# Small operations off VectorE, a re-ordered head and bracketed 64-row tails in a transformer block on one core

## The chip, the core and the metric

The kernel runs on one core of a Trainium2 chip. The metric is the device time of one execution in microseconds (us); lower is better. The core has five engines that run side by side, each with its own queue that it works through in order: TensorE (PE in the profile, its weight loads PEld), VectorE (DVE), ScalarE (ACT), GpSimd (POOL) and SyncE (SP), which here issues nearly all DMA transfers.

## The reference

The input is x, 2048 rows of 576. A block with attention and a feed-forward network is computed in two halves, each behind a layer norm and with a residual.

```
h  = x + A(layernorm(x))                 # A: 32 heads of 18, 4 segments of 512 rows
h2 = h + gelu(layernorm(h) @ w1 + b1) @ w2 + b2      # w1: 576 x 4608
# in A, for each segment s, with q, k, v of that segment:
p    = softmax(q k^T * 18**-0.5, causal inside the segment)
dot  = p @ v
mem  = (phi(q) @ M) / (phi(q) @ z + 1e-6)    # phi(t) = t+1 if t>0 else exp(t)
o    = g * mem + (1-g) * dot                 # g = sigmoid(beta), per head
M   += phi(k)^T v ;  z += sum of phi(k)      # for the next segment
A    = concat(o) @ wo
```

Data are bfloat16; sums are kept in float32.

## The kernel before

The rows are worked in 8 chunks of 256, each of two tiles of 128 rows. A segment is two chunks. Per tile: the layer norm (`layernorm`, L725 to L760) has its statistics, a sum and a product on DVE (L729, L733 to L735), a power on POOL (L740) and the application on DVE or ACT (L743, L748). The normalised tile `xn1` is transposed to `xT`, on PE for the first two tiles (L761) and by a transposing DMA after that (L491). Four projections of 432 columns, each five matmuls (L722 for the four full rows of 128, L723 for the rest of 64 rows and a row of zeros), give Q, K and V, which ACT or DVE copies out of PSUM (L844 to L854). Q and K are transposed in turn (L874 on PE, else L491).

The attention (`stream_A`) goes in 80 visits. A visit runs 16 score matmuls of 32 rows, four at a time on PE (L957), into the four-bank tile `st4`; ACT takes the exponential of all 128x2048 (L974); POOL masks the blocks on the diagonal (L978); later PE multiplies with V (L997) into the bank `ox`, and DVE and POOL finish (L1043 to L1053). From the second segment on, the memory is recalled (`memory_in`, `memory_mm`, L1011 to L1034) from `MZ_blk`, which DVE makes from the sums `MZacc` (L933, L936). `stream_B` multiplies with wo, adds the residual, norms again to `xn2` (with a copy of its last 64 columns, L745) and transposes to `xn2T`.

The feed-forward part is two streams. `stream_F1` takes w1 in groups of 512 columns (`load_w1`), 9 groups per chunk and 72 in all, in two buffers `w1g` (the first five groups lie elsewhere too). A group of 128 columns of the hidden layer over 256 rows is five matmuls: four with 128 rows (L722) and one with the last 64 rows and a row of zeros (L723), which runs in full mode like the others. Its sum is evicted with the bias by DVE or ACT (`evict`, L1286 and L1284), and gelu is taken by ACT over many at once (L1349), with a table load when ACT comes from the exponential. `stream_F2` multiplies with w2 (L1376). A `Pair` is another form of the same work: two halves of a w1 group, whose four 64-row rests (`tail`, L1214) run two at a time in the upper and lower half of PE, put ahead of a visit's scores, since PE changes its tile mode there anyway; the full parts (`main`, L1220) follow. PE's banks are three plus, before and after the attention, `ox`.

The order of all of it is made when the program is built. Each piece of work is an `op` on an engine with an assumed duration and a due time (`SLACK`, `PHASES`, and the recorded due times `LATE`); `step` plays through time, and on each engine begins the ready operation that is due first:

```
can = [o for o in queue[e] if o.ready() <= now and not (e == "SP" and waits_for_queue(o))]
if can:
    begin(min(can, key=lambda o: (o.due, o.made)))
```

PE takes what the streams offer. Where PE would have nothing to do early on (`WARM`, the first 62 us of the plan), a matmul of zeros is put in (L1424), which then stands in PE's queue like any other. On the chip the queues run in that fixed order and wait for each other by semaphores. `either` chooses between DVE and ACT for an eviction by what each has queued.

Of the kernel before, what the change touches and what calls it, by code (L numbers as in the profile page):

```python
# [8 lines left out]
ACT = mybir.ActivationFunctionType  # L9
# [7 lines left out]
def kernel(  # L17
# [41 lines left out]
    def sbuf(name, shape, dt=BF16):  # L59
# [13 lines left out]
    SLACK = dict(head=2.35, lnp=15.71, lnb=4.06, pow=-3.98, apply=7.94, ek_k=78.96, relu_k=-8.71, min_k=3.71,  # L73
                 add_k=10.93, mz=14.56, exp=16.96, ek=21.6, relu=47.98, min=14.06, add=31.72, hb=57.84,
                 gelu=30.88, finish=-1.23, mem=0.08, sum=20.21, out=3.91, hd=34.06, xp=-29.81, xb=-19.31,
                 t_x=23.19, t_q=37.57, t_k=38.16, t_o=-3.03, t_h=19.9, w1=3.76, w2=33.77, hc=-2.46, evict=-17.31,
                 qk=7.8, ot=-7.54, mask=0.42, lead=1.57, balance=22.63, b1=11.77, zeros=6.77, hold=0.62,
                 delay=0.92, pe_x=2, pe_q=3, pe_k=2, pe_o=2, pe_h=1, d_x1=1.69, d_wk=-5.24, marg=0.8, cj=4,
                 flex=1.0, qkv=0.0, flexn=1.0, d_wv=1.68, d_xb=0.5, d_wo=3, d_b2=1.97, bulk=11.07, w2v=5)
    PHASES = [(30.0, dict(exp=38.12, hold=2.18, sum=8.51, lnp=15.18, min_k=9.68, lead=1.93, t_h=47.5, t_o=-3.5,  # L80
                          flexn=1.85, mem=25.71)),
              (60.0, dict(gelu=28.89, apply=7.66, min_k=-36.61, lnp=16.16, w2=14.91, qk=8.17, t_q=37.57, delay=0,
                          hc=9.3)),
              (110.0, dict(t_x=30.47, min=14.15, mz=13.94, hold=5.27, w1=24.51, t_q=28.42, ek=20.74, apply=0.43,
                          pow=-9.03, xp=-16.35, hc=0.85, w2=31.47, out=4.0, bulk=8.26)),
              (200.0, dict(mem=-1.42, w1=12.55, lead=3.33, t_o=-5.89, mask=8.5, finish=-0.41, xb=-20.35, hd=32.92,
                          lnb=4.83, exp=20.2, apply=21.55)),
              (300.0, dict(add_k=6.54, delay=0.17, add=4.0, hd=24.4, mem=3.13, mz=15.86, ek_k=80.69, min_k=14.3,
                          exp=16.63, join=-18.57, qk=4.56, lead=1.87, xp=-30.24, min=9.66, qkv=5.33, t_x=21.9,
                          out=37.08, apply=10.19, hold=0.28))]  # L90
# [81 lines left out]
    def note(o, rd, wr):  # L172
# [5 lines left out]
        for k in rd:  # L178
# [4 lines left out]
        'wqkv0': [0.2],  # L183
        'mhalf': [4.1],
        'wqkv_pad': [4.4],
# [14 lines left out]
        ('x_p', 0): [0, 15.2, 41.5, 77.3, 169.5, 193.4, 233.4],  # L200
        ('qk', 0, 'pad'): [17.5],
        'wqkv1': [1.4],
        ('v1', 0): [22.7],
        ('v1', 1): [26.9],
        'ident': [4.9],
        ('v1', 2): [45.5],
        ('v1', 3): [57.3],
        'wqkv1t': [1],
        ('v1', 4): [60.2],
        ('v1', 5): [67.5],  # L210
        'maskcol': [58.4, 70.6, 62.4, 71.3, 63.8],
        ('qk', 2, 'pad'): [24.9],
        ('x_p', 1): [2, 26.1, 91.6, 103.7, 202.6, 212.6, 294.4],
        ('v1', 6): [123.5],
        'beta': [29.3],
        'wqkv2': [3.5],
        'wqkv2t': [3.7],
        ('o', 0, 'pad'): [27.9],
        ('x_b', 0): [7.6, 30.5, 71.9, 119, 172.9, 230.9, 273.1, 317.9, 377.7],
        ('phik', 0, 'pad'): [32.7],  # L220
        ('wo', 4): [38.2, 44],
        ('phik', 1, 'pad'): [33.8],
        ('w1', 0, 'z', 0): [41.5],
        ('x_b', 1): [10.9, 45, 87.4, 133.1, 201.2, 242.8, 296.4, 330.6, 418],
        ('w1', 0, 'z', 1): [39.6],
        'stp0': [2.8, 3.3, 3.8, 4.3, 11, 11.5, 11.9, 12.5, 21.5, 23.3, 21.5, 22.3, 51.2, 47.3, 36.4, 25.7,
            78.9, 94.5, 95.4, 97.9, 174.1, 174.5, 175, 175.5, 195.3, 194.5, 193.8, 196.7, 244.8, 239.6,
            247.2, 236.5],
        ('w1', 1, 'z', 0): [44.9],
        'b1': [18.1],  # L230
        ('w1m', 2, 'z', 1): [46.3],
        ('wo', 0): [23.5],
        ('w1m', 2, 'z', 0): [59],
        ('w1', 1, 'z', 1): [53.3],
        ('qk', 3, 'pad'): [57.8],
        ('o', 1, 'pad'): [48.3],
        ('xn1', 0): [5, 13.2, 25.8, 49.4, 89.7, 176.2, 197.5, 238.4],
        ('w1m', 3, 'z', 1): [58.4],
        ('w1m', 3, 'z', 0): [58.7],
        ('w1m', 4, 'z', 1): [66],  # L240
        ('xT', 'p', 0): [5.2, 16.9, 22.9, 46.4, 90.3, 177.4, 198.5, 245.7],
        'MZb': [71.1, 69, 72.3, 71.4, 71.7, 76.8, 64.6, 74.2, 62.6, 191.3, 192.4, 192.2, 195.4, 196.6, 197.4,
# [1240 lines left out]
```

## Time and profile before

| | |
|---|---|
| time, median of 3 runs | 478.51 us (477.85 to 479.26) |
| the profiled execution: time | 476.5 us |
| its span | 474.8 us, 14410 instructions |
| busy DVE, ACT, POOL | 311.4, 302.9, 217.2 us |
| matmuls on PE | 6056, of these 76 fillers with zeros |
| granted PE clock | 1.00 |
| HBM read, written | 60.09 MB, 7.08 MB |

The profile is of one execution. A group of its table 5 reads: line, engine, operation, output and input tiles, shapes, count | busy time in us, mean of one in ns | idle time of the engine before them and what ended it. In the timeline, a row is start, length, engine, line, operation, count and, in brackets, idle time before it. Matmuls are pipelined: a row's length is longer than the time until the next can start.

### The profile page before, as it was taken

The page shows a single profiled execution, that of the slowest core. Times are in us where ns is not written, and L with a number is a line of the kernel's source. Part 1 is how long each engine was busy: PE and PEld are TensorE (multiplying, and loading weights), DVE is VectorE, ACT ScalarE, POOL GpSimd, SP SyncE. Part 2 cuts the span into 40 slices and gives each one's busy share as a digit, 9 for nine tenths or more (in the row PEclk, how much of TensorE's full clock was granted, in tenths as well). Part 3 has the DMA queues.
Part 4 walks back from the last instruction along what each step waited for, and adds up shares of the span by engine and source line. Part 5 has one row for each costly group of instructions (what it writes and reads, how often), then busy time and mean ns, then how long its engine had stood idle before and what let it go on. Part 6 is the DMA issues. An engine that isn't in the chain of part 4 may idle for free.

```text
span 474.8 us, 14410 instructions
## 1 busy us (share of the span) xinstructions
PE 462.5 (97%) x6056; PEld 350.9 (74%) x6056; DVE 311.4 (66%) x744; ACT 302.9 (64%) x245; POOL 217.2 (46%) x333
## 2 busy tenths in 40 slices
PE   8999999799999999999999999999999999999997
PEld 6655687468777777767768777777877788888875
DVE  4889996587877476888877556887457646334310
ACT  2578879964678668896789595687457864212210
POOL 9468463295745344786773518665133312000000
PEclk9999999999999999999999999999999999999999
DMA  8999799927588577469458559486744655655411
GB/s 240 200 231 206 262 163 295 253 52 165 162 214 218 150 178 185 97 142 199 83 155 204 156 143 193 89 196 187 181 147 135 185 166 158 185 168 164 137 39 50
DMA packets 118881, 79.94 MB, mean 168 GB/s; under 512 B 53344, under 2 KB 116768, under 8 KB 118816
## 3 DMA queue, kind: packets, MB, share of 16 engines
q1 hardware_dynamic: 118784, 79.01, 66.8%
q8 instruction: 47, 0.77, 0.7%
q14 instruction: 18, 0.15, 0.1%
q0 software_dynamic: 32, 0.01, 0.1%
HBM read 60.09 MB, written 7.08 MB: 141 GB/s over the span
## 4 chain that ended last, share of the span: by engine, by line
PE 84%; DVE 6%; ACT 4%; issue 2%; DMA 2%; SPq 1%; ACTq 0%; DVEq 0%
PE bank L722 29%; PE bank L1376 26%; PE bank L723 7%; PE st L957 5%; PE ox L997 4%; PE bank L1220 4%; PE ox L1376 3%; PE st L1424 2%; DMA xT<-xn 2%; ACT pt L974 1%; PE ox L722 1%; PE bank L1026 1%; ACT hT L1349 1%; DVE ox L1043 1%; PE bank L1214 1%
## 5 line engine op out<-in xcount | busy, mean ns | idle before, releaser
L974 ACT ACTIVATE pt<-st 128x2048 bf16<-128x2048 f32 x80 | 150.2, 1877 | 65.4 <-PE st L957 63.6
L1376 PE MATMUL bank<-w_sb,hT 128*128 128x288 bf16 x1044 | 144.0, 286 | 2.1 <-ACT hT L1349 2.1
L1286 DVE TENSOR_TENSOR hT<-bank,b1T 128x512 bf16<-128x512 f32 x130 | 89.3, 688 | 72.5 <-PE bank L723 65.1
L1376 PEld LDWEIGHTS <-hT 128*128 128x128 bf16 x1152 | 110.5, 98 | 31.8 <-ACT hT L1349 2.4
L978 POOL TENSOR_SCALAR_AFFINE_SELECT pt<-pt 128x512 bf16<-128x512 bf16 x128 | 80.4, 643 | 107.1 <-ACT pt L974 105.4
L722 PE MATMUL bank<-xn2T,w1g 128*128 128x256 bf16 (+1 forms) x888 | 122.2, 269 | 1.9 <-DMA w1g<-in_B_w_dram 0.9
L722 PEld LDWEIGHTS <-w1g 128*128 128x128 bf16 x944 | 88.4, 98 | 16.3 <-issue 1.5
L1349 ACT ACTIVATE hT<-hT 128x4608 bf16<-128x4608 bf16 (+5 forms) x23 | 66.0, 2874 | 46.7 <-DVE hT L1286 46.5
L723 PE MATMUL bank<-xn2T,w1g 128*128 128x256 bf16 (+1 forms) x222 | 59.7, 269 | 0.0
L722 PE MATMUL bank<-wqkv,xT 128*128 128x432 bf16 x256 | 57.4, 346 | 1.1 <-DMA xT<-xn 0.8
L722 PEld LDWEIGHTS <-xT 128*128 128x128 bf16 x384 | 34.9, 97 | 23.7 <-DMA xT<-xn 0.9
L1016 POOL TENSOR_TENSOR pq<-ek,pq 128x512 bf16<-128x512 bf16 x24 | 27.9, 1163 | 11.8 <-DVE ek L1014 9.1
L957 PE MATMUL st<-QT,KT 32*128 32x128 bf16 x1280 | 32.2, 217 | 1.2 <-ACT pt L974 1.1
L1043 DVE STREAM_TRANSPOSE ox<-ox 128x512 f32<-128x512 f32 x32 | 23.2, 725 | 11.7 <-PE ox L997 11.1
L1380 DVE TENSOR_TENSOR ot<-bank,hc 128x288 bf16<-128x288 f32 x29 | 13.1, 453 | 25.1 <-PE bank L1376 25.1
L957 PEld LDWEIGHTS <-KT 32*128 32x128 bf16 x1280 | 18.8, 92 | 14.3 <-issue 9.2
L997 PE MATMUL ox<-pt,v_aug 128*19 128x128 bf16 x1280 | 26.5, 220 | 0.0
L997 PEld LDWEIGHTS <-v_aug 128*19 128x19 bf16 x1280 | 17.9, 91 | 10.9 <-issue 10.0
L723 PEld LDWEIGHTS <-w1g 128*128 128x128 bf16 x236 | 23.1, 98 | 2.7 <-DMA w1g<-in_B_w_dram 0.2
L844 ACT CAST qk_pad<-bank 128x432 bf16<-128x432 f32 x28 | 14.5, 522 | 14.3 <-PE bank L723 11.8
L1053 POOL TENSOR_TENSOR o_nat<-t,t 128x288 bf16<-128x288 f32 x24 | 19.6, 816 | 8.3 <-DVE t L1052 7.5
L723 PE MATMUL bank<-wqkv,xT 65*128 65x432 bf16 x64 | 22.2, 348 | 0.0
(124 smaller groups left out, 578.1 us busy)
## 6 DMA issues: line engine op xcount, KB each, us to landing
w1g<-in_B_w_dram SPq DMA_DIRECT2D x67, 512.0 KB, 4.3
w_sb<-in_B_w_dram SPq DMA_DIRECT2D x6, 864.0 KB, 6.9
hd<-h_t SPq DMA_DIRECT2D x16, 288.0 KB, 3.5
hc<-hd SPq DMA_DIRECT2D x32, 144.0 KB, 3.4
w1g<-in_B_w_dram SPq DMA_DIRECT2D x134, 32.0 KB, 3.5
x_b<-in_A_x_dram SPq DMA_DIRECT2D x18, 144.0 KB, 4.4
hT<-in_B_w_dram SPq DMA_DIRECT2D x5, 512.0 KB, 4.8
out_dram<-ot SPq DMA_DIRECT2D x16, 144.0 KB, 1.8
```

The lines of the kernel that those rows point to most:

```text
L722: nc.tensor.matmul(out=out_ap, lhsT=lhsT_of(slice(0, P), k), rhs=rhs_of(slice(0, P), k), start=(k == 0), stop=False)
L723: nc.tensor.matmul(out=out_ap, lhsT=lhsT_of(slice(0, rest), 4), rhs=rhs_of(slice(0, rest), 4), start=False, stop=True)
L957: nc.tensor.matmul(out=st4[:, i, n * P:(n + 1) * P], lhsT=KTs[(2 * (c - c % 2) + kt) % NK][rows, g, :], rhs=QTs[(2 * c + qt) % NQ][rows, g ...
L974: op("ACT", 1.88, lambda: nc.scalar.activation(out=pt[:], in_=st4[:], func=ACT.Exp, scale=scale), sk, [("pt", slot, n) for n in range(4)], ...
L978: op("POOL", 0.65, lambda n=n: nc.gpsimd.affine_select(out=pt[:, :, n * P:(n + 1) * P], in_=pt[:, :, n * P:(n + 1) * P], pattern=[[0, 4], ...
L997: nc.tensor.matmul(out=ox[32 * i:32 * i + E, (g % 4) * P:(g % 4) * P + P], lhsT=v_augs[(2 * s0 + kt) % NV][:, G * i + g, :], rhs=pts[slot] ...
L1016: op("POOL", 1.16, lambda: nc.gpsimd.tensor_tensor(out=pq[:], in0=e_g, in1=pq[:], op=ALU.add), ["ek"], ["pq"], slack=due("add"))
L1043: op("DVE", 0.73, lambda: nc.vector.transpose(out=ox[:], in_=ox[:]), [], ["ox"], slack=slack)
L1053: op("POOL", 0.8, lambda: nc.gpsimd.tensor_tensor(out=o_dst, in0=t1[:].rearrange("p (g b) e -> p g b e", g=4), in1=t2[:].rearrange("p (g b ...
L1286: either((0.684, lambda: nc.vector.tensor_tensor(out=dst, in0=acc, in1=bias, op=ALU.add)), (nj * (0.166 + w * 0.00082), by_act), [b, "b1T" ...
L1349: op("ACT", (f1e - f0) * Q * 0.00083 + 0.18, lambda hT=hT, f0=f0, f1e=f1e: nc.scalar.activation(out=hT[:, f0:f1e, :], in_=hT[:, f0:f1e, :] ...
L1376: nc.tensor.matmul(out=acc, lhsT=hT[:, q, tl * P:(tl + 1) * P], rhs=w2_sb[:, q, hs], start=(q == 0), stop=(q == NF - 1))
```

## The change

The diff rewrites much of the order, by new values in `SLACK`, `PHASES` and `LATE`. The edits of substance are these:

- *Layer norm.* The sum with eps goes to POOL, in one step with the power; the product for ACT is made on POOL only where ACT applies. The application can go to POOL, DVE or ACT (for `xn1`) or to DVE or ACT (for `xn2`); the 64-column copy of `xn2` goes to POOL or ACT. The transposed tile's copy out of PSUM goes to DVE or ACT, before always to ACT.
- *Memory.* `MZacc` starts from zeros with 1e-6 in one row per head, so the addition of 1e-6 on DVE before each reciprocal is left out; `MZ_blk` is made with four operations, not eight, and `maskcol` is gone.
- *Head.* The second tile of x, the weights and beta are loaded in another order (beta by SP, before by POOL); the third tile of x and the fourth Q are transposed on PE too.
- *Look-ahead.* An engine other than SP leaves a ready operation waiting when one that is due more than 1 us earlier becomes ready within `look` and the first would not be done by then.
- *Tails.* After the last scores the four banks of `st4` join the others. A `Pair` can then have up to six halves, and its 12 tails run in one bracket of their own (`pair.tails` as one op in mode half). For the last 18 groups of w1 there are five buffers, three of them in the projections' weights `wqkv`, which are spent by then. In the built orders there are 132 tails (before 40), 72 of them in six such brackets.
- *gelu.* A function of its own, called in the first chunk's first part too.

```diff
 def layernorm(...):
-    def first():
-        nc.vector.bn_aggr(out=mv[:], in_=stats[:])
-        nc.vector.tensor_scalar(out=rstd[:], in0=mv[:, 1:2], scalar1=EPS, scalar2=None, op0=ALU.add)
-        nc.vector.tensor_scalar(out=nmr[:], in0=mv[:, 0:1], scalar1=-1.0, scalar2=None, op0=ALU.mult)
+    def power():
+        nc.gpsimd.tensor_scalar(out=rstd[:], in0=mv[:, 1:2], scalar1=EPS, scalar2=None, op0=ALU.add)
+        nc.gpsimd.tensor_tensor(out=rstd[:], in0=rstd[:], in1=mhalf[:], op=ALU.pow)
...
-    if behind("ACT") + due("flexn") < behind("DVE"):
...
-    op("DVE", 0.80 if f32 else 0.50, apply, ...)
+    waiting = {"DVE": behind("DVE"), "ACT": behind("ACT") + due("flexn")}
+    if not f32:
+        waiting["POOL"] = behind("POOL") + due("flexp")
+    by = min(waiting, key=waiting.get)
...
+    elif by == "POOL":
+        op("POOL", 0.70, lambda: apply(nc.gpsimd), ["st" + who, skey], [dkey], slack=late)
...
+    if f32:
+        if behind("ACT") + due("flexd") < behind("POOL"):
+            op("ACT", 0.22, lambda: nc.scalar.copy(out=dst[:, D:XW], in_=dst[:, 512:D]), ...)
+        else:
+            op("POOL", 0.2, lambda: nc.gpsimd.tensor_copy(out=dst[:, D:XW], in_=dst[:, 512:D]), ...)
...
 SLACK:
-    pe_x=2, pe_q=3, ... d_x1=1.69, d_wk=-5.24
+    pe_x=3, pe_q=4, ... d_x1=1.39, d_wk=11.96, d_beta=12.99, flexp=-4.78, flexd=4.34, look=0.3, wide=6, gp0=18
...
+    for j in range(4):
+        banks["st", j] = st4[:, j, :]
...
 def w1_of(n):
+    if n >= W0:                      # W0 = (NCH - 2) * NG = 54
+        j = (n - W0) % 5
+        if j > 1:
+            return w1_late[j - 2], ("w1l", j)
...
 def memory_mm(...):
-    op("DVE", 0.175, lambda: nc.vector.tensor_scalar(out=r2[:], in0=omv[:, :, Dh], scalar1=1e-6, scalar2=None, op0=ALU.add), ...)
-    op("DVE", 0.25, lambda: nc.vector.reciprocal(out=r2[:], in_=r2[:]), ...)
+    op("DVE", 0.25, lambda: nc.vector.reciprocal(out=r2[:], in_=omv[:, :, Dh]), ...)
...
 class Pair:
-    def __init__(self, c, jp, keys):
-        self.halves = [Half(f_slots.take(), c, jp + i) for i in range(2)]
+    def __init__(self, c, jp, keys, n=2):
+        self.halves = [Half(f_slots.take(), c, jp + i) for i in range(n)]
+    def tails(self):
+        for i in range(0, len(self.halves), 2):
+            for a in range(2):
+                for half in self.halves[i:i + 2]:
+                    half.tail(a)
...
 def stream_F1():
+    if ("st", 0) in bank_slots.free:
+        count = min(SLACK["wide"], NF // 2 - jp, 6 if c * NG >= W0 else 4 if jp % 2 == 0 else 2)
+    if count > 1 and count % 2 == 0:
+        yield need(lambda: go_on() and loaded.issuperset(groups), f_slots, keys, n=count)
+        pair = Pair(c, jp, keys, count)
+        op("PE", 0.12 * count, pair.tails, keys, [h.b for h in pair.halves], mode="half")
...
 def step():
-    begin(min(can, key=lambda o: (o.due, o.made)))
+    o = min(can, key=lambda o: (o.due, o.made))
+    if e != "SP":
+        soon = [p for p in queue[e] if p.due < o.due - 1 and now < p.ready() <= now + due("look")]
+        if soon:
+            t = min(p.ready() for p in soon) + 0.03
+            can = [p for p in can if now + p.dur <= t]
+            if not can:
+                continue
+            o = min(can, key=lambda o: (o.due, o.made))
+    begin(o)
```

More of the change, by code (lines that the diff above doesn't have):

```diff
@@ L72 @@
     PVS = 2
[L73 to L83, printed above, removed]
-              (110.0, dict(t_x=30.47, min=14.15, mz=13.94, hold=5.27, w1=24.51, t_q=28.42, ek=20.74, apply=0.43,
[L85 to L90, printed above, removed]
+    SLACK = dict(head=12.38, lnp=16.71, lnb=23.55, pow=-3.88, apply=7.94, ek_k=75.47, relu_k=-7.78, min_k=3.71,
+                 add_k=9.07, mz=13.76, exp=14.23, ek=22.53, relu=44.54, min=-5.65, add=31.72, hb=57.84,
+                 gelu=36.38, finish=-1.23, mem=0.08, sum=20.02, out=3.91, hd=34.06, xp=-16.29, xb=-24.97,
+                 t_x=8.86, t_q=32.3, t_k=38.16, t_o=-3.03, t_h=19.9, w1=15.02, w2=33.77, hc=-4.28, evict=-17.31,
+                 qk=6.88, ot=-6.3, mask=0.42, lead=2.7, balance=30.12, b1=12.01, zeros=1.99, hold=0.78,
+                 delay=1.78, pe_x=3, pe_q=4, pe_k=2, pe_o=2, pe_h=1, d_x1=1.39, d_wk=11.96, marg=0.78, cj=4,
+                 flex=1.0, qkv=-2.87, flexn=1.0, d_wv=2.17, d_xb=0.5, d_wo=6.32, d_b2=0.41, d_beta=12.99,
+                 flexp=-4.78, flexd=4.34, look=0.3, wide=6, gp0=18, bulk=11.07, w2v=3)
@@ L683, in constants @@
             memset("DVE", 0.14, v_augs[j][:, :, Dh:E], 1.0, ("v1", j), slack=4)
-        memset("DVE", 0.09, maskcol[:], 0.0, "maskcol", slack=5)
-        for i in range(4):
-            memset("DVE", 0.09, maskcol[32 * i:32 * i + Dh, :], 1.0, "maskcol", slack=5)
         for j in range(2, 4):
@@ L696, in constants @@
         memset("POOL", 0.95, MZ_blk[:], 0.0, "MZb", slack=7)
+        memset("POOL", 0.6, MZacc[:], 0.0, "MZacc", slack=8)
+        for i in range(4):
+            memset("POOL", 0.11, MZacc[32 * i:32 * i + E, :, E * i + Dh:E * i + E], 1e-6, "MZacc", slack=8)
+            memset("POOL", 0.11, MZacc[32 * i:32 * i + Dh, :, E * i + Dh:E * i + E], 0.0, "MZacc", slack=8)
+        memset("POOL", 0.11, gmz[:, :, Dh:E], 1.0, "gmz", slack=8)
     def gates():
@@ L747, in apply_by_act @@
-        def apply_by_act():
-            nc.scalar.activation(out=dst[:, 0:D], in_=src, func=ACT.Identity, bias=nmr[:], scale=rstd[:])
-            if f32:
-                nc.scalar.copy(out=dst[:, D:XW], in_=dst[:, 512:D])
-        if behind("ACT") + due("flexn") < behind("DVE"):
-            op("POOL", 0.2, lambda: nc.gpsimd.tensor_tensor(out=nmr[:], in0=nmr[:], in1=rstd[:], op=ALU.mult), [], ["st" + who], slack=slack + due("pow"))
-            op("ACT", 0.86 if f32 else 0.64, apply_by_act, ["st" + who, skey], [dkey], slack=slack + due("apply"))
-            return
@@ L756, in layernorm, with apply @@
-        op("DVE", 0.80 if f32 else 0.50, apply, ["st" + who, skey], [dkey], slack=slack + due("apply"), port=True)
+        op("DVE", 0.22, lambda: nc.vector.bn_aggr(out=mv[:], in_=stats[:]), [], ["st" + who], slack=slack)
+        op("POOL", 0.78, power, ["mhalf"], ["st" + who], slack=slack + due("pow"))
+        def apply(e):
+            e.tensor_scalar(out=dst[:, 0:D], in0=src, scalar1=mv[:, 0:1], scalar2=rstd[:], op0=ALU.subtract, op1=ALU.mult)
+        late = slack + due("apply")
+        waiting = {"DVE": behind("DVE"), "ACT": behind("ACT") + due("flexn")}
@@ new lines, in layernorm @@
+        if not f32:
+            waiting["POOL"] = behind("POOL") + due("flexp")
+        by = min(waiting, key=waiting.get)
+        if by == "ACT":
+            op("POOL", 0.22, lambda: nc.gpsimd.tensor_scalar(out=nmr[:], in0=mv[:, 0:1], scalar1=rstd[:], scalar2=-1.0, op0=ALU.mult, op1=ALU.mult),
+               [], ["st" + who], slack=slack + due("pow"))
+            op("ACT", 0.64, lambda: nc.scalar.activation(out=dst[:, 0:D], in_=src, func=ACT.Identity, bias=nmr[:], scale=rstd[:]),
+               ["st" + who, skey], [dkey], slack=late)
+        elif by == "POOL":
+            op("POOL", 0.70, lambda: apply(nc.gpsimd), ["st" + who, skey], [dkey], slack=late)
+        else:
+            op("DVE", 0.62 if f32 else 0.55, lambda: apply(nc.vector), ["st" + who, skey], [dkey], slack=late, port=True)
@@ L758, in transposes5 @@
+        if f32:
+            if behind("ACT") + due("flexd") < behind("POOL"):
+                op("ACT", 0.22, lambda: nc.scalar.copy(out=dst[:, D:XW], in_=dst[:, 512:D]), [], [dkey], slack=late, tag="again")
+            else:
+                op("POOL", 0.2, lambda: nc.gpsimd.tensor_copy(out=dst[:, D:XW], in_=dst[:, 512:D]), [], [dkey], slack=late, tag="again")
     def transposes5(src, bank):
@@ L776, in when @@
                 t = NEVER
[L777 removed]
+                if (cond is None or cond()) and (slots is None or len(slots.free) >= n):
                     t = ready("PE", rd, wr)
                     if slots is not None and t < NEVER:
[L780 removed]
+                        t = max(t, slots.when(n))
                 seen = changes, t
@@ L883, in stream_P @@
                     gates()
+                if c == NCH - 1:
+                    for n in range(W0 + 2, W0 + 5):
+                        for h in range(2):
+                            memset("POOL", 0.3, w1_of(n)[0][64 - 64 * h:P - 64 * h, 4, 256 * h:256 * h + 256], 0.0,
+                                   (*w1_of(n)[1], "z", h), slack=due("zeros"), more=WALL)
+                        load_w1(n, WALL)
     def stream_K(tl):
@@ L962, in go @@
             if pair is not None:
-                for a in range(2):
-                    for half in pair.halves:
-                        half.tail(a)
+                pair.tails()
             for n in range(4):
@@ L1135, in stream_A @@
         bank_slots.free.append("ox")
+        for i in range(4):
+            bank_slots.free.append(("st", i))
     def stream_B(tl):
@@ L1295, in stream_F1, with gelu @@
             f0 = 0
+            def gelu(c, f0, f1e, hT=hT):
+                alone = NCH - 1 in done_A
+                if f1e - f0 < (6 if alone else 18 if c else SLACK["gp0"]) and f1e < NF:
+                    return f0
+                op("ACT", (f1e - f0) * Q * 0.00083 + 0.18, lambda: nc.scalar.activation(
+                    out=hT[:, f0:f1e, :], in_=hT[:, f0:f1e, :], func=ACT.Gelu_apprx_tanh),
+                   [], [("hT", c % 2, q) for q in range(f0 // 2, f1e // 2)], slack=0 if alone else due("gelu"), table="gelu")
+                return f1e
             if c == 0:
```

360 lines of the change are left out of this document (192 added, 168 removed), and 310 rows, old and new, of the table LATE.

## The prediction

> **What bounds the kernel now.** I read the page first, then the busy times by stretches, the matmuls one after another in the timeline, the groups by shape, and last the chain of waits in the first 100 us.
>
> ```profile
> span 474.8 us, 14410 instructions
> PE 462.5 (97%) x6056; PEld 350.9 (74%) x6056; DVE 311.4 (66%) x744; ACT 302.9 (64%) x245; POOL 217.2 (46%) x333
> ```
>
> TensorE (PE) is busy almost throughout, so the question is what fills its time. A busy PE can be a PE that runs fillers or drains between tile modes, so I split the 474.8 us myself. Start to start, a matmul takes 0.0555 us for 128 columns, 0.109 for 256, 0.1225 for 288 and 0.183 for 432 (four score or value matmuls share one slot, two 64-row tails likewise). Summed over the 5980 matmuls that do work this gives 420.6 us. A change of tile mode adds 0.092 us (after a score group the next matmul starts 0.147 later instead of 0.055); 236 changes are 21.7 us. The 76 filler matmuls with zeros (L1424) take 11.2, PE starts at 1.3, and 3.5 us follow its last matmul. What is left, some 16.4 us, is waiting, and of that some 0.3 us in each 20 us is only the grain of this sum.
>
> ```profile
> 0.00:10.00 10.00, 8.67 (x54) 6.32 (x55) 4.15 (x25) 3.08 (x4) 8.99 (x24) 1.00 0.80 232
> 40.00:50.00 10.00, 9.19 (x147) 5.20 (x148) 9.49 (x25) 9.45 (x12) 6.84 (x10) 1.00 1.13 231
> 50.00:60.00 10.00, 9.76 (x202) 6.78 (x203) 9.68 (x24) 7.85 (x8) 4.85 (x8) 1.00 0.76 256
> 70.00:90.00 20.00, 17.82 (x288) 13.93 (x287) 11.16 (x24) 17.96 (x13) 5.71 (x9) 1.00 1.06 298
> 400.00:420.00 20.00, 20.00 (x175) 16.90 (x173) 7.89 (x14) 4.72 (x4) 1.29 (x1) 1.00 0.67 198
> ```
>
> Columns: stretch, length, busy time of PE, PE's weight loads, DVE, ACT, POOL, granted clock, DMA share, GB/s. From 100 us on PE does nothing but work (400 to 420: my sum leaves 0.05 us). Before that there are two other bounds: DVE and ACT at 9.5 of 10 us around 45 us, ACT at 18 of 20 around 80.
>
> ```profile
> 1.33 5.61 PE L1424 MATMUL st<-pq 128*128 128x256 bf16 x26 [1.33 <-DVE pq L669]
> 8.93 2.13 PE L1424 MATMUL st<-pq 128*128 128x256 bf16 x18
> 91.02 0.42 PE L1376 MATMUL bank<-w_sb,hT 128*128 128x288 bf16 x2
> 93.53 0.42 PE L1376 MATMUL bank<-w_sb,hT 128*128 128x288 bf16 x2 [2.09 <-ACT hT L1349]
> 144.07 0.39 PE L1214 MATMUL bank<-xn2T,w1g 64*128 64x256 bf16 x4
> 144.40 0.40 PE L957 MATMUL st<-QT,KT 32*128 32x128 bf16 x16
> 22.88 6.12 DMA xT<-xn
> ```
>
> The first two rows are fillers (the first 26 at 0.216 us each, later ones at 0.109); the next two show PE waiting for the second gelu; then four tails that cost 0.33 us until the scores; the last row (from the chain) is a transposing DMA that PE waits for. PE's loss (start, fillers, waits) by visit of the attention (one group of 16 score matmuls is a visit, 80 in all), is: 11.2 us up to the first scores at 20.0, 2.9 to visit 4 (32.5), 2.9 to visit 18 (74.1), 5.5 to visit 22 (98.3), 6.4 to the end. Less the grain, 2.7 + 2.3 + 5.2 + 0.8 = 11.0 us are waits that could go, beside the head.
>
> **The change, part by part.** The sum is made against the profiled execution: span 474.8, time 476.5 us. The median of the runs is 478.5, so 2.0 goes on top at the end.
>
> *The tails.* The orders of instructions of the two kernels show 40 tails before and 132 after: 60 in 15 score visits (before 10) and 72 in six brackets of 12 behind the last scores. So 92 matmuls of 64 or 65 rows leave full mode, where each took 0.109, and share slots: 92 x 0.0545 = 5.0 us less. The mode changes rise from 236 to 248 (22 more at tails, 10 fewer elsewhere): 12 x 0.092 = 1.1 more. A bracket by itself: 12 x 0.109 = 1.31 becomes 0.65 + 2 x 0.092 = 0.84. Thirteen more transposes run on PE (third tile of x, Q of the fourth): 13 x 0.0555 = 0.7 more. PE's own time: -5.0 + 1.1 + 0.7 = **-3.2 us**. This lies on the path, since nothing else fills PE after 100 us. Its conditions are covered: a bracket wants six of eight free banks, so six evictions, 6 x 0.688 = 4.1 us of DVE, have to end under the 48 to 72 second-layer matmuls between brackets (5.9 to 8.8 us); and three weight groups, which five buffers now hold (three of them in the spent QKV weights), at 198 GB/s as before. Without that cover a bracket would wait up to 4.1 us, six times; DVE's 7.9 of 20 us there speaks against it.
>
> *Off DVE.*
>
> ```profile
> L734 DVE TENSOR_SCALAR rstd_p<-mv_p 128x1 f32<-128x1 f32 x16 | 2.5, 154 | 0.6
> L735 DVE TENSOR_SCALAR nmr_p<-mv_p 128x1 f32<-128x1 f32 x16 | 2.3, 144 | 0.0
> L936 DVE TENSOR_SCALAR MZ_blk<-MZacc,maskcol 32x8 bf16<-32x8 f32 x12 | 4.6, 382 | 0.1
> L895 POOL TENSOR_SCALAR phik_pad<-qk_pad 128x576 bf16<-128x576 bf16 x10 | 6.7, 674 | 0.7 <-DVE qk_pad L847 0.7
> L978 POOL TENSOR_SCALAR_AFFINE_SELECT pt<-pt 128x512 bf16<-128x512 bf16 x128 | 80.4, 643 | 107.1 <-ACT pt L974 105.4 <-DVE r L1044 1.4 <-DVE hT L1286 0.2
> ```
>
> DVE loses 32 x (0.154 + 0.144) = 9.5, 18 layer norm applications at 0.64 to 0.66 = 11.7, 16 copies at 0.427 = 6.8, 12 x 0.382 = 4.6, 24 additions at 0.167 = 4.0, three evictions 2.1 and 0.4 of memsets: 39 us. It gains 3 copies of xT at about 0.6 (between 0.31 and 0.69, the nearest rows), 15 evictions of Q, K, V that ACT did (7.2) and one QT copy 0.7: 10. Net -29 of 311 us, but only what falls before 100 us can matter: by the sixth finished block (about 55 us) some 5.6 us. ACT is relieved by as much there (QKV copies, xT copies; by the tenth exponential 5.5 us). POOL takes 32 small operations (no such row; between 0.19 as L753 and 0.55 as L740; I take 0.2, being plain arithmetic as L753), 15 applications (between 0.67 as L895 and 1.2 as L899; I take 0.7, one input tensor), 15 copies and six products at about 0.2, and 3.3 of memsets: +24 us, up to +50 at the upper ends, on 217; some 6 us of it in the first 60.
>
> [...] L745, a copy of 64 columns on DVE, takes 0.181 at best and 1.055 at worst in this trace; L743 0.39 to 1.35. Over L743, L745, L897 and L1014 the means lie 14.0 us above the minima in sum; at 12.23 us, with POOL idle, L743 takes 0.43, at 15.29, beside L895, 0.88. [...] In my sum this costs nothing, since 34 of these 81 operations leave DVE with the change; what it gives when it does cost is a rival below.
>
> *Head.* x's second tile moves from sixth to third transfer, ahead of Wk. Before, its layer norm waited 3.5 us for it (statistics at 9.68), and the projections stood at 8.0, 10.9, 13.5. After, 51 fillers and both transposes come first, then seven projections in a row. Fillers: 26 x 0.216 + 25 x 0.109 = 8.3, so the projections begin near 10.4, bounded below by the tail of Wq, which moves behind Wk (1512 KB; 1584 KB had landed at 9.6 before). Wv, now after 2376 KB, lands near 12.8 (792 KB more than what was there at 9.6, at the 252 GB/s of the second 10 us), under the fourth projection (14.1). First scores: loss 1.3 + 8.4 for 52 fillers = 9.8 against 11.2: **-1.4**, with 0.4 us more work done. If Wq's tail or POOL's memsets (2.6 us before the second apply) are 1.4 late, this is nothing.
>
> *Waits.* To visit 4: the third tile is transposed on PE, so one transposing DMA on SP's queue instead of two precedes the fourth; 2.7 becomes some 1.5. To visit 18: 15 fillers now stand in the order behind visit 6 (1.6 us, spent whether needed or not); with 0.9 beside them 2.5, as before. To visit 22: before, PE ran dry behind gelus of 4.9 and 3.2 us with their table loads (1.28 each way). After, the first (4.5) has 66 first-layer and 8 second-layer matmuls behind its scores (8.2 us), the second (3.6) 40 projections and 28 second-layer ones (10.8 us): I take 1.5 for 5.2. Rest as before. Sum 6.3 against 11.0: **-4.7**. The look-ahead has no price of its own; it works only through these orders.
>
> 476.5 - 3.2 - 1.4 - 4.7 = 467.2; with the 2.0, **469.2 us**.
>
> **Rivals.** (B) *The waits stay*: PE's own 4.6 us arrive, DVE's relief is eaten. For it: POOL's 6 us in the first 60 equal DVE's 5.6, and an operation stretched as in L745 hands them over one for one. Against: ACT is relieved too. 476.5 - 4.6 + 2.0 = 473.9. [...] (C) *All waits go*, but for the 16 fillers still queued (1.7): 476.5 - 4.6 - 11.0 + 1.7 + 2.0 = 464.6. For it: both engines that bound the first 100 us lose a tenth of their work there. Against: each wait has another cause. (A) *POOL becomes the pace*, slower: a layer norm's 1.45 us on POOL now queues with the masks (0.643 each), and values wait for masks. POOL is busy 26.9 of the 40 us from 20 to 60 and comes to 33; its queue decides once it has no gap left, at some 40, which the upper ends of its prices reach. If each of the 14 visits from 4 to 18 then lasts one mask longer, +9.0 with no wait recovered: 476.5 - 4.6 + 9.0 + 2.0 = 482.9. (D) *Nothing comes of it*: brackets waiting for banks or weights give back the 4.6: 478.5. That the brackets are not built at all is excluded by the order of instructions.
>
> **How the numbers follow.** Forecast 0.47 (its own range 466 to 472.5, by 3 us either way in the waits), B 0.21, C 0.15, A 0.12, D 0.05. A measurement here tells 0.3% (1.4 us) from no change. Faster: 0.47 + 0.21 + 0.15 = 0.83; same 0.05; slower 0.12. The range holds forecast, B and C with 2 to 3 us around the outer two: 462 to 477.
>
> **What would show it.** Right: six groups of 12 tails after the last scores with no wait ahead of them; fillers ending near 10 us; first scores near 19; no 2 us gap at the gelus; DVE below 9 of 10 us at 45. Wrong: waits of values or of the layer norm for POOL between 30 and 75 us (A); DVE operations longer than before (B); waits ahead of a bracket for a bank or for weights (D).

## The result: slower by 2.4%, for two reasons

| | before | after |
|---|---|---|
| time, median (4 runs each) | 478.65 us | 489.45 us (489.42 to 491.89) |
| ratio, 95% interval | 1 | 1.0239 (1.0204 to 1.0274) |
| the profiled execution: time, span | 476.5, 474.8 us | 489.46, 487.7 us |

The forecast was 469.2 us (462 to 477), so the time lies outside the range and on the other side. From the page of the kernel after, its span, the busy times and the first line of its chain:

```profile
span 487.7 us, 14341 instructions
PE 461.6 (95%) x6060; PEld 346.0 (71%) x6060; DVE 291.4 (60%) x621; ACT 297.8 (61%) x235; POOL 265.4 (54%) x413
PE 79%; POOL 9%; DVE 6%; ACT 2%; issue 2%; DMA 1%; SPq 0%; POOLq 0%; ACTq 0%; DVEq 0%
```

POOL, which had no share in the first line of the chain before, now has 9% of it. POOL gained 48 us of busy time, twice the forecast's 24; DVE lost 20. Busy time by stretches, kernel after (same columns as in the prediction):

```profile
0.00:10.00 10.00, 6.11 (x34) 4.37 (x35) 4.30 (x21) 1.87 (x2) 8.79 (x23) 0.89 0.82 233
20.00:30.00 10.00, 9.19 (x134) 5.74 (x133) 9.45 (x24) 6.31 (x8) 9.91 (x13) 1.00 0.55 120
30.00:40.00 10.00, 8.60 (x154) 5.55 (x155) 7.83 (x18) 7.22 (x8) 9.26 (x15) 1.00 1.16 278
40.00:50.00 10.00, 9.83 (x144) 5.73 (x133) 6.79 (x19) 8.28 (x9) 9.81 (x13) 1.00 0.73 217
70.00:90.00 20.00, 19.47 (x384) 16.43 (x382) 13.78 (x28) 15.69 (x8) 11.97 (x17) 1.00 0.91 233
400.00:420.00 20.00, 18.67 (x171) 14.95 (x170) 7.13 (x11) 2.97 (x2) 0.00 (x0) 1.00 0.39 115
```

Three things are to be seen. At 40 to 50 us DVE fell from 9.49 to 6.79, as intended, but POOL, the fifth busy time, has hardly a gap between 20 and 50. At 70 to 90 PE gained what the forecast put on the gelus (17.82 before). And at 400 to 420, where PE had been busy for 20.00 of 20, it is busy for 18.67.

Two places of the timeline of the kernel after show why, the head and the stretch behind a bracket, and two groups of its table go with them:

```profile
5.42 2.31 POOL L771 TENSOR_SCALAR xn<-x_p,mv_p,rstd_p 128x576 bf16<-128x576 bf16 x1
7.79 0.65 PE L796 MATMUL bank<-ident,xn 128*128 128x128 bf16 x5 [2.59 <-POOL xn L771]
11.11 2.30 POOL L771 TENSOR_SCALAR xn<-x_p,mv_p,rstd_p 128x576 bf16<-128x576 bf16 x1
```

```profile
385.51 0.39 PE L1249 MATMUL bank<-xn2T,w1g 64*128 64x256 bf16 x4
391.52 0.65 PE L1437 MATMUL st<-w_sb,hT 128*128 128x288 bf16 x4
392.96 4.57 PE L1437 MATMUL st<-w_sb,hT 128*128 128x288 bf16 x36 [0.78 <-DVE hT L1327]
398.08 2.12 PE L1437 MATMUL st<-w_sb,hT 128*128 128x288 bf16 x16 [0.55 <-DVE ot L1441]
```

```profile
L771 POOL TENSOR_SCALAR xn<-x_p,mv_p,rstd_p 128x576 bf16<-128x576 bf16 x14 | 32.4, 2313 | 0.9
L1437 PE MATMUL st<-w_sb,hT 128*128 128x288 bf16 x324 | 42.4, 286 | 6.4 <-DVE hT L1327 3.1
```

A layer norm application on POOL takes 2.31 us, not the 0.7 of the sum, and in the head PE stands still for it. The row shows the 14 on `x_p`; one more is on `x_b` (2.31 us too), so POOL has the 15 that the prediction counted. The chain lies on POOL alone from 31.0 to 51.2 us, with three applications among its masks and other work. The bracket at 385.51 starts without a wait, as forecast; it is the work behind it, in the banks `st`, that waits for evictions. Start to start I find 13 such gaps behind the last scores, each 0.71 or 0.94 us longer than the matmul, 10.6 us in sum. Ten are ahead of second-layer matmuls (L1437), three between the full parts of first-layer ones (L1255). The group by line has 6.4, since its rows count a matmul's modelled tail as busy.

The working of the prediction can be made again for each kernel: PE's loss (start, fillers, waits, with the grain left in) in us, by visit. The columns "own banks", "DVE applies" and "both" are experiments told below.

| | before | forecast | after | own banks | DVE applies | both |
|---|---|---|---|---|---|---|
| up to the first scores | 11.2 | 9.8 | 13.4 | 13.4 | 11.1 | 11.1 |
| to visit 4 | 2.9 | 1.7 | 1.6 | 1.6 | 1.4 | 1.4 |
| to visit 18 | 2.9 | 3.1 | 8.7 | 8.1 | 4.5 | 4.9 |
| to visit 22 | 5.5 | 1.8 | 0.2 | 0.3 | 1.1 | 0.3 |
| to the last scores | 5.9 | 5.9 | 9.9 | 11.3 | 8.7 | 7.1 |
| behind them | 0.2 | 0.2 | 11.1 | 0.4 | 11.1 | 0.3 |
| sum | 28.6 | 22.5 | 44.9 | 35.1 | 37.9 | 25.1 |

Beside the loss stands PE's own time, matmuls and mode changes: 420.5 + 21.7 before, 416.2 + 22.9 after, 3.1 less (forecast 3.2). The loss grew by 16.3.

### The profile page after: what moved, and what is told of

Read it like the earlier page. It is cut to its first block, busy times and chain, and to the rows that moved or that the text cites. A ratio compares the mean times of both kernels' runs of the same rounds, so it can differ in the third digit from the quotient of the medians.

```text
span 487.7 us, 14341 instructions
## 1 busy us (share of the span) xinstructions
PE 461.6 (95%) x6060; PEld 346.0 (71%) x6060; DVE 291.4 (60%) x621; ACT 297.8 (61%) x235; POOL 265.4 (54%) x413
## 4 chain that ended last, share of the span: by engine, by line
PE 79%; POOL 9%; DVE 6%; ACT 2%; issue 2%; DMA 1%; SPq 0%; POOLq 0%; ACTq 0%; DVEq 0%
PE bank L751 21%; PE bank L1437 19%; PE bank L1255 8%; PE st L1437 8%; PE bank L752 5%; PE st L993 4%; PE ox L1031 4%; POOL xn L771 3%; PE st L1255 3%; POOL pt L1012 2%; PE bank L1249 1%; ACT pt L1008 1%; PE ox L1255 1%; DMA xT<-xn 1%; PE bank L1060 1%
## 5 line engine op out<-in xcount | busy, mean ns | idle before, releaser
L1437 PEld LDWEIGHTS <-hT 128*128 128x128 bf16 x1152 | 110.7, 98 | 36.7 <-issue 8.3
L1437 PE MATMUL bank<-w_sb,hT 128*128 128x288 bf16 x792 | 111.5, 286 | 0.0
L1327 DVE TENSOR_TENSOR hT<-bank,b1T 128x512 bf16<-128x512 f32 x112 | 77.0, 688 | 56.7 <-PE bank L1255 35.3
L1342 ACT ACTIVATE hT<-hT 128x1536 bf16<-128x1536 bf16 (+3 forms) x24 | 66.3, 2763 | 71.2 <-DVE hT L1327 71.1
L751 PE MATMUL bank<-xn2T,w1g 128*128 128x256 bf16 (+1 forms) x568 | 76.8, 267 | 1.1 <-DVE v_aug L890 0.6
L751 PEld LDWEIGHTS <-w1g 128*128 128x128 bf16 x576 | 52.7, 98 | 9.7 <-issue 1.1
L751 PE MATMUL bank<-wqkv,xT 128*128 128x432 bf16 x248 | 55.5, 346 | 1.0 <-DMA xT<-xn 0.6
L1437 PE MATMUL st<-w_sb,hT 128*128 128x288 bf16 x324 | 42.4, 286 | 6.4 <-DVE hT L1327 3.1
L1255 PEld LDWEIGHTS <-w1g 128*128 128x128 bf16 x368 | 34.4, 98 | 6.2 <-issue 0.6
L752 PE MATMUL bank<-xn2T,w1g 128*128 128x256 bf16 (+1 forms) x142 | 37.9, 267 | 0.0
L1255 PE MATMUL bank<-xn2T,w1g 128*128 128x256 bf16 x296 | 36.1, 273 | 0.0
L771 POOL TENSOR_SCALAR xn<-x_p,mv_p,rstd_p 128x576 bf16<-128x576 bf16 x14 | 32.4, 2313 | 0.9
L1031 PEld LDWEIGHTS <-v_aug 128*19 128x19 bf16 x1280 | 18.2, 91 | 13.4 <-issue 12.1
```

The source lines that it names most:

```text
L751: nc.tensor.matmul(out=out_ap, lhsT=lhsT_of(slice(0, P), k), rhs=rhs_of(slice(0, P), k), start=(k == 0), stop=False)
L752: nc.tensor.matmul(out=out_ap, lhsT=lhsT_of(slice(0, rest), 4), rhs=rhs_of(slice(0, rest), 4), start=False, stop=True)
L771: e.tensor_scalar(out=dst[:, 0:D], in0=src, scalar1=mv[:, 0:1], scalar2=rstd[:], op0=ALU.subtract, op1=ALU.mult)
L1031: nc.tensor.matmul(out=ox[32 * i:32 * i + E, (g % 4) * P:(g % 4) * P + P], lhsT=v_augs[(2 * s0 + kt) % NV][:, G * i + g, :], rhs=pts[slot] ...
L1255: nc.tensor.matmul(out=self.acc[:, a, :], lhsT=self.wt[:, k, f:f + P], rhs=xn2T[self.c % 4][:, k, :], start=False, stop=(k == 3), skip_gro ...
L1327: either((0.684, lambda: nc.vector.tensor_tensor(out=dst, in0=acc, in1=bias, op=ALU.add)), (nj * (0.166 + w * 0.00082), by_act), [b, "b1T" ...
```

## The experiments

Theory: (1) the application on POOL costs 2.31 us and loses the time ahead of visit 18; (2) behind the last scores the brackets wait for nothing that is real: `st4` is one tile of four banks, and a matmul into one bank waits for the eviction of another bank of the same tile. In the built program such waits are there, for matmuls whose own bank has long been read. Rivals: the new order itself loses the time, whoever applies; the waits for banks are real or come from the hardware. Each time below is a median; behind it stands the ratio to the kernel before with its 95% interval.

**Without POOL's option** (`e1_no_pool_apply`)

```diff
-        if not f32:
-            waiting["POOL"] = behind("POOL") + due("flexp")
```

> The changed kernel, but the layer norm's application is never given to GpSimd (the choice is between VectorE and ScalarE). Theory (the slow application): 15 applications of 2.31 us on GpSimd, planned at 0.70, hold up the head and the visits to 75 us; without them the loss to the first scores falls from 13.4 to about 10, the loss to visit 18 from 23.7 to 15 or 17, nothing changes behind the last scores (waits there stay near 11 us): 480 us (477 to 483) for 489.5. [...]

Measured: 497.59 us, 1.0393 (1.0339 to 1.0447), slower than after. A miss, and the fault is the experiment's. The planner makes another order of all the work once the option is gone (20 applications go to DVE, 12 to ACT). The loss up to visit 18 did fall, to 16.3 from 23.7, but visits 51 to 66 (228 to 307 us) now lose 11.6, where after loses 2.0, in waits of several kinds; weights come late there, for instance (timeline):

```profile
274.52 0.70 PE L751 MATMUL bank<-xn2T,w1g 128*128 128x256 bf16 x4 [1.38 <-DMA w1g<-in_B_w_dram]
```

Nothing follows from its time. An edit that isolates has to keep the order.

**Without the banks for the brackets** (`e2_no_st_banks`)

```diff
-        for i in range(4):
-            bank_slots.free.append(("st", i))
```

> The changed kernel, but the four banks of the score tile are not given to the feed-forward part after the last scores, so there are no brackets of 12 tails either. Theory (false waits between the banks of one tile): the waits behind the last scores fall from 11.2 us to about 1, the 72 tails go back to full mode (+2.8): 482 us (480 to 484). Rival (the burst of evictions or the weights are late by themselves): the same, so this run only says how much the whole part is worth; the next two tell them apart. If the brackets pay as built, the time rises to 492.

Measured: 481.96 us, 1.0087 (1.0059 to 1.0114). As expected: without brackets, 7.5 us come back. So the brackets and the four extra banks, with all they save, cost that much here.

**The same memory as four tiles** (`e4_own_banks` on top of `e1`, `e5_own_banks_only` on top of after). The pool of `st4` is closed after the last exponential, and four tiles of one bank each take its place; the order of the instructions stays.

```diff
-    banks["st", j] = st4[:, j, :]
+    banks["st", j] = Late(lambda j=j: st_bank(j))
```

> As the first run of this set (no application on GpSimd), and the score tile's memory is given back after the last exponential and taken again as four tiles of one bank each, so that a matmul into one bank does not wait for a read of another. The order of the instructions is that of the first run. Theory (false waits): the waits behind the last scores fall from about 11 to about 1.5 us, 10 us less than the first run: 470 us (467 to 473). Rival (evictions or weights late by themselves): within 2 us of the first run, about 480.

> The changed kernel with only the score tile's memory split into four tiles of one bank each after the last exponential; the applications stay on GpSimd. Theory (false waits): 479.5 us (478 to 482), the time up to the last scores as in the changed kernel (about 360 us), waits behind them about 1.5 us. Rival (evictions or weights late by themselves): 488 or more. If the two causes add up, the gain over the changed kernel equals that of own banks over the run without GpSimd's applications, within 1 us.

Measured: `e4` 485.8 us, 1.015 (1.01 to 1.0201), missed in the absolute with the `e1` it stands on, but 11.8 below that; `e5` 479.81 us, 1.0035 (1.001 to 1.0061), 9.6 below after. Had the two causes simply added, these two gains would agree within 1 us; they are 2.2 apart. The loss behind the last scores fell from 11.1 to 0.4 (column "own banks"). Nearly all of that wait was between different banks.

**The wait by itself** (`e11_bank_waits`, `e13_bank_waits_ordered`). First half with `one[:, n % 4, :]`, a tile of four banks; second half with `four[n % 4]`.

```
for n in range(16):
    for k in range(4):
        nc.tensor.matmul(out=one[:, n % 4, :], lhsT=xt[:, 0:P], rhs=xt[:, 0:512], start=(k == 0), stop=(k == 3))
    nc.vector.tensor_tensor(out=y[n % 4][:], in0=one[:, n % 4, :], in1=xt[:, 0:512], op=ALU.add)
```

> Leaves out the whole computation: 16 times four matmuls of 512 columns into one bank and an eviction of that bank by VectorE (128x512, the form that takes 0.69 us), four banks in turn, first with one tile of four banks, then with four tiles of one bank. Theory (matmuls into one bank of a tile wait for the eviction of another bank of the same tile): in the first half a round is matmuls 0.86 plus eviction 0.69 plus the signals, about 1.8 us, and every round shows a wait of PE for VectorE; in the second half a round is 0.86, without waits. Rival (the waits come from the hardware, a bank or port that both use): both halves the same.

> As the run of the same 32 rounds before it, whose two halves had been woven into each other, but with the order kept: first all 16 rounds on the tile of four banks, then 16 on four tiles of one bank. Leaves out the whole computation. Theory (matmuls into one bank of a tile wait for the eviction of another bank of it): a round of the first half lasts 0.86 for the matmuls, 0.69 for the eviction and some 0.2 for the signals, about 1.8 us, with a wait of PE for VectorE of 0.7 to 1.0 in each; a round of the second half 0.86 and no wait. Rival (the hardware makes them wait): both halves the same.

In `e11` the two halves were woven into each other, so that the one's matmuls filled the other's waits (PE shows none for VectorE): inconclusive. `e13` kept the order; its timeline (PE), two rounds of the first half and the whole second:

```profile
37.39 1.86 PE L68 MATMUL one<-xt 128*128 128x512 bf16 x4 [0.78 <-DVE y L69]
40.04 1.86 PE L68 MATMUL one<-xt 128*128 128x512 bf16 x4 [0.78 <-DVE y L69]
44.35 15.85 PE L72 MATMUL four<-xt 128*128 128x512 bf16 x64
```

Every one of 15 rounds waits 0.78 us for the eviction of the bank before; with four tiles there is no wait in 16 rounds. Four banks each and the same evictions (692 ns in both halves), so the hardware does not ask for it. A round lasted 2.65 us instead of the expected 1.8, because the matmuls themselves ran at half pace (0.427 us each, in most of the second half 0.216; below).

**POOL's applications issued on DVE, order kept** (`e6_apply_dve`; `e7_dve_and_banks` with the four tiles as well)

```diff
-            op("POOL", 0.70, lambda: apply(nc.gpsimd), ...)
+            op("POOL", 0.70, lambda: apply(nc.vector), ...)
```

> The kernel after, in its own order; only the 14 layer norm applications that GpSimd got are issued on VectorE at the same places. Theory 1 (the 2.31 us of an application on GpSimd, against about 0.6 on VectorE, lose what was lost before the last scores): the loss up to visit 18 goes from 23.7 us to about 17, as in the kernel before, the head's fillers end near 10 us, and the time falls by 6 to 8 us to 482 (481 to 484); the waits behind the last scores, some 10 us, stay. Rival (the new order itself loses it, whoever applies): within 2 us of the kernel after, 488 to 490. Second rival (GpSimd slows VectorE's instructions while it applies): as theory 1 in time, but VectorE's own instructions become shorter too; in the kernel after those that lie beside an application are not longer than the others.

> As the previous run, and the memory of the four-bank tile is given to four tiles of one bank each after the last exponential. Theory (the two causes are separate and add): the run with own banks alone took 479.8 us; less the 6 to 8 us of the applications this gives 472 to 474, faster than the kernel before (477.5) by about 1%. Rival (the two overlap, or the order itself loses the rest): 478 to 480.

All 15 applications were moved. Measured: `e6` 482.53 us, 1.0077 (1.0055 to 1.01), 6.9 below after; `e7` **470.65 us, 0.9824 (0.9786 to 0.9863)**, faster than both kernels and a little below the 472 to 474 expected. The two gains do not simply add: with the four tiles the applications are worth 9.2 us, with the application on DVE the tiles 11.9. The difference of 2.2 us lies mostly between visit 22 and the last scores (table above) and was not followed. Of `e6`'s 7.0 us of regained loss 2.3 are in the head and 4.2 between visits 4 and 18. In the head 30 fillers ran at 0.213 us in after and 16 in `e6`, but that did not set the time: in after the last filler of the head started at 13.01, and the transposes waited for the second application (11.11 to 13.41) until 13.47. The second rival of `e6` does not explain the 6.9 us: over 59 DVE instructions that ran beside an application in the kernel after, the time above the mean of the same instruction elsewhere sums to 0.1 us; ten evictions (L1327), for instance, took 0.690 in the mean, elsewhere 0.688. Only four of the 59 are operations between bfloat16 tiles in SBUF, the kind that the prediction saw stretched; one of these took 0.71 us, where the same takes 0.27 to 0.29 with POOL idle. From the page of `e7`, and then from its timeline (its lines are some 24 higher):

```profile
PE 457.2 (98%) x6060; PEld 345.2 (74%) x6060; DVE 297.8 (64%) x636; ACT 297.9 (64%) x235; POOL 232.1 (50%) x398
```

```profile
5.37 1.59 DVE L795 TENSOR_SCALAR xn<-x_p,mv_p,rstd_p 128x576 bf16<-128x576 bf16 x1 [1.23 <-POOL rstd_p L787]
7.01 0.28 PEld L820 LDWEIGHTS <-xn 128*128 128x128 bf16 x5 [1.74 <-DVE xn L795]
7.02 0.45 PE L820 MATMUL bank<-ident,xn 128*128 128x128 bf16 x5 [1.27 <-POOL MZacc L667]
389.96 0.39 PE L1273 MATMUL bank<-xn2T,wqkv 64*128 64x256 bf16 x4
395.97 4.21 PE L1461 MATMUL stb<-w_sb,hT 128*128 128x288 bf16 x33
```

Behind the bracket 33 second-layer matmuls run without a gap. What is left in the head is a wait for the first application on DVE. It took 1.59 us beside five memsets of POOL (0.42 is the median of these operations in `e6`) and ended at 6.96; the transposes, whose weight load reads `xn`, began 0.06 later. The profile puts the matmul's wait down to the memset of `MZacc`, which the transposes do not read.

**POOL's application in the kernel before** (`e9_before_pool_apply`)

```diff
-        op("DVE", 0.80 if f32 else 0.50, apply, ...)
+        op("DVE", 0.50, on_pool, ...)          # for xn1: nc.gpsimd.tensor_scalar, the same operands
```

> The kernel before, in its own order; only its 13 layer norm applications of the attention part that VectorE did are issued on GpSimd at the same places. Theory 1 (each costs 2.31 us instead of 0.6, the head's in full and those up to visit 18 in part): first scores about 1.7 us later or more, loss to visit 18 up by 5 to 8 us, time 482 to 486. Rival (the place in the new order loses it, not the duration): within 2 us of the kernel before, 476 to 479.

Measured: 490.68 us, 1.0237 (1.0201 to 1.0273). The direction is theory 1's, the size beyond its range: 13 applications alone cost 11.6 us, as much as the whole change. In its source view:

```profile
L758 POOL TENSOR_SCALAR xn<-x_p,mv_p,rstd_p x11: 2281/2291/2448, 6.0 to 229.2; 128x576 bf16<-128x576 bf16 x11
```

Its loss exceeds that of before by 3.7 us at the first scores, 8.1 at visit 18 and 13.2 at the end, so the price is not paid in the early visits only.

**What in the application costs** (`e8_pool_forms`)

> Leaves out the whole computation: one tile is loaded, its statistics made, and GpSimd then works through one form after another, three of each, on 128x576 bfloat16. Theory (scalars read from memory, one per partition, are what costs): subtract and multiply by two such scalars 2.31 us; min and max, or subtract and multiply, with constants 0.67; one such scalar, alone or with a constant, near 2.3 or between; 288 columns with two scalars 1.2, 64 columns 0.3. Rival 1 (the arithmetic costs, not the scalars): subtract and multiply with constants takes 2.31 too. Rival 2 (the neighbours cost: contention with VectorE or a wait inside the instruction): all two-scalar forms here, alone on the core, are at 0.7.

Groups of its table, three of each form; in the order shown: two scalars from memory, one from memory and a constant, two constants (subtract, multiply), one scalar with multiply alone, two scalars on 288 columns, VectorE with two scalars, two constants (min, max), two scalars on 64 columns. The last line is from the source view of VectorE's three:

```profile
L75 POOL TENSOR_SCALAR y<-xt,mv,rstd 128x576 bf16<-128x576 bf16 x3 | 6.8, 2292 | 0.1
L85 POOL TENSOR_SCALAR y<-xt,mv 128x576 bf16<-128x576 bf16 x3 | 6.6, 2211 | 0.0
L79 POOL TENSOR_SCALAR y<-xt 128x576 bf16<-128x576 bf16 x3 | 6.3, 2136 | 0.1
L81 POOL TENSOR_SCALAR y<-xt,rstd 128x576 bf16<-128x576 bf16 x3 | 5.1, 1723 | 0.0
L87 POOL TENSOR_SCALAR y<-xt,mv,rstd 128x288 bf16<-128x288 bf16 x3 | 3.9, 1322 | 0.0
L95 DVE TENSOR_SCALAR y<-xt,mv,rstd 128x576 bf16<-128x576 bf16 x3 | 2.0, 726 | 42.6 <-POOL y L93 42.6
L77 POOL TENSOR_SCALAR y<-xt 128x576 bf16<-128x576 bf16 x3 | 1.9, 666 | 0.0
L89 POOL TENSOR_SCALAR y<-xt,mv,rstd 128x64 bf16<-128x64 bf16 x3 | 1.7, 578 | 0.0
L95 DVE TENSOR_SCALAR y<-xt,mv,rstd x3: 416/420/1343, 46.5 to 48.1; 128x576 bf16<-128x576 bf16 x3
```

The theory of this run fell. Constants instead of scalars from memory save 0.16 us of 2.29; it is subtract and multiply in place of min and max that make 2.14 out of 0.67. Rival 1 was right. That POOL's instruction runs with VectorE idle and still takes 2.29 rules out rival 2. VectorE's row of 726 ns is a mean of unlike ones: the first of the three ran beside two copies on POOL and took 1.34 us, the other two, with POOL done, 0.42.

**What the brackets are worth** (`e10_dve_no_brackets`: `e6` with the edit of `e2`)

> The kernel after with its 14 GpSimd applications issued on VectorE, and without the four banks for the brackets, so that no bracket of 12 tails is built. It tells what the brackets are worth once their waits are gone. Theory (a bracket saves 1.31 - 0.84 = 0.47 us of PE, six of them 2.8, as the prediction had it): 2.8 us more than the 470.7 of the run with own banks, 473 to 475. Rival (extra banks are worth something beyond the tails, or the application and the brackets interact): below 472 or above 476.

Measured: 474.06 us, 0.9894 (0.9866 to 0.9921), as expected. It is 3.4 us above `e7`. PE's own time is 442.1 us against 439.3 of `e7`: 2.8 us, the sum's 6 x 0.47; but both are counted with the same times per matmul, so this is no measurement of its own. The trace of `e7` is one: each of its six brackets takes 0.76 us from its first tail to the next matmul, and that first tail comes 0.10 later than a second-layer matmul would: 0.86 for the sum's 0.84.

**Without the late fillers** (`e12_no_late_fillers`: the 15 fillers behind visit 6 are not issued)

```diff
-                   lambda: nc.tensor.matmul(out=dst, lhsT=pq[:, 0, :], ...)
+                   (lambda: nc.tensor.matmul(out=dst, lhsT=pq[:, 0, :], ...)) if now < 25 else (lambda: None)
```

> As the run with own banks and VectorE's application (470.7 us), but the 15 filler matmuls behind the sixth visit are not issued. Theory 1 (they stand in front of real work, 1.65 us): 469.0 to 469.5. Rival (PE would wait there in any case, as the prediction's sum to visit 18 assumed): 470.2 to 471.2. If the clock is granted lower without them, above 471.2.

Measured: 472.5 us, 0.9881 (0.9832 to 0.9931); the interval overlaps that of `e7`, so the times do not tell them apart. The timeline does: where the fillers stood, PE now waits.

```profile
39.28 0.90 PE L775 MATMUL bank<-wqkv,xT 128*128 128x432 bf16 x4 [1.21 <-DMA xT<-xn]
```

From visit 6 to visit 10 the loss is 1.6 us instead of 1.8. The fillers covered a wait for the transposing DMA, as the rival said.

## Why the prediction was wrong, step by step

- *The application on POOL* is the first step that failed. It was priced at 0.7 us "between 0.67 as L895 and 1.2 as L899; I take 0.7, one input tensor". The nearest row was the wrong one: L895 is min and max with constants. It measured 2.31, beyond both ends, 15 times: 24.2 us more on POOL, which is all of the 24 that its busy time came out above the forecast. This is the mechanism of rival A, POOL as the pace. POOL was busy 36.6 us of the 40 from 20 to 60 (forecast 33), less than the 40 that A asked for, but over 9.2 of 10 in three of the four stretches, and for 20 us the chain did not leave it. With DVE in its place 6.9 us come back.
- *"Its conditions are covered"* is the second, and worth more: 9.6 us (11.9 with DVE applying). The cover was counted right. There were free banks, DVE had time, no weights were late, and no bracket waited. But the sum asked whether six evictions fit under the second-layer matmuls and not whether matmuls may run beside the evictions, when both use banks of one tile. Matmuls waited 13 times, 0.71 or 0.94 us each. Rival D named waits about the brackets at 4.6 us; it had the place, neither the cause nor the size.
- *Head.* Forecast -1.4; after +2.2, of it 2.3 the application on POOL (`e6`). Without that it is still only -0.1: PE waited 1.27 us for the first application, which took 1.59 us on DVE beside POOL's memsets. The prediction had said that those memsets, 1.4 late, would make the gain nothing; the effect is of that size, but they were not late, the operation beside them was long.
- *Waits.* To visit 4 right (1.6 for 1.7). To visit 18 wrong in after by the application; without it still 1.8 more than forecast ("both"), though the fillers in it hide a wait. At the gelus better than forecast: 0.2 of 1.8 left. From visit 22 to the last scores 1.2 more than before remain with both causes mended; this was not followed further.
- *PE's own time* was right: -3.1 for -3.2, and the bracket's term of 0.84 measured 0.86 in `e7`.
- *Off DVE.* Forecast 29 us less; busy time fell by 20.0, and the durations, which overlap and are what the sum added, by 26.4. The ten applications to `xn2` that stayed on DVE took 0.86 us in the mean, 0.64 before: rival B's sign, an operation made longer, is there, but small beside the two costs.
- *The sum.* With both causes taken away the change takes 470.65 us where 469.2 was forecast. Two costs were missing from the sum; that the rest comes so near is in part luck. By the table "both" loses 1.3 us more than forecast in the head, 1.8 to visit 18 and 1.2 to the last scores, and 1.5 less at the gelus. The stretch of DVE operations beside POOL, weighed there by L743 and L745, did not decide the result: the 59 instructions told of with `e6` lost 0.1 us in all beside an application. It does bear on what is left: the 1.59 us in the head, where 0.42 is the median, and the 1.34 against 0.42 in `e8`. What causes it no run shows.

## What to carry to other kernels

Price an operation that moves to another engine by a row with the same arithmetic on that engine, not by one with the same shape; where there is none, measure one alone before moving 15 of them. When buffers that used to be one tile are handed out singly, give each a tile of its own: on the one tile of `e13`, PE waited 0.78 us in each of 15 rounds while VectorE read another bank than the one PE wrote next, and on four tiles not once. Where a wait is put down to a tile that the waiting instruction does not read, look at the other engines it waits for. And when an order made by a planner is tested, change the engine or the memory under the fixed order; taking an option away makes another kernel.

## What was not expected of the hardware

- On GpSimd, 128x576 bfloat16 takes 0.67 us with min and max or as a copy, 1.72 with one multiply or subtract, 2.29 with both; 578, 1322 and 2292 ns for 64, 288 and 576 columns are some 0.37 us and 3.3 ns a column. VectorE took 0.42 for both with POOL idle (`e8`, and the median in `e6`), 1.34 beside POOL's copies and 1.59 beside its memsets.
- In the first half of `e13` matmuls of 512 columns started every 0.427 us, in the second every 0.216 after the first nine, 5.5 us after the last pause. PE, which paused 0.78 of every 2.65 us in the first half, thus ran at half pace throughout it, though the column of the granted clock reads 1.00 there. In `e11`, without the pauses, the pace doubled 3.4 us after the first matmul, from some 0.42 us a matmul to 0.22. No run shows what sets the pace. The waits behind the brackets did not halve it: 13 in some 85 us, and the 36 matmuls of the row at 392.96 kept 0.122 us.
- The fillers' pace varies from run to run: in the head 19 fillers ran at 0.213 us in `e7`, 34 in `e12`, in the same order, and the first scores came 1.2 us later. The pace is halved as in `e13`, but both had the same pause of 1.7 us among the fillers, so what made the difference is not shown.
